# Two blocks of a feed-forward layer regrouped into one seven-product matrix scheme, with a fixed order by half step on VectorE, ScalarE and the DMA queue

## Chip, cores and metric

The kernel runs on one core of one Trainium2 chip. The metric is device microseconds of an execution. One profiled execution comes with its span, from the first to the last instruction.

## What is computed

A chunked attention over 4 x 8 heads with 768 positions of 64 (chunks of 32 queries, each against 8 memory keys and 56 neighbours) gives 3072 tokens of 512 features. Two feed-forward layers follow, in 32-bit floats:

```python
x = attention(q, k, v, mem_k, mem_v)          # 3072 x 512
h = x @ w_in                                  # 512 x 2048
g = maximum(h, 0) + log1p(exp(-abs(h)))       # softplus
x = g @ w_out                                 # 2048 x 512
h = x @ w_in2
g = h - tanh(h)
out = g @ w_out2
```

## The kernel before, in words

**Numbers.** Every operand of the feed-forward products is split into a high part, rounded to the format that TensorE takes at full rate (fp32r), and a low rest. A product is three matmuls, high-high, high-low and low-high (`mm3`, L307). Splitting costs a cast on ScalarE and a subtraction on VectorE per tile.

**Attention.** A unit is 128 tokens; there are 24. `s_mm` (L202) makes scores, `softmax` (L217) normalises, `t_mm` (L251) transposes, `t_out` (L259) copies the transposes, `v_mm` (L265) multiplies by values, `x_out` (L280) splits the result into an x tile. All units share the PSUM tile ps_a.

**Layer one** works on six blocks j of 512 tokens. For each of 16 slices f of the 2048 features, `ff_h` (L316) makes h with 12 matmuls into one of two banks ps_h, `chain1` (L332) takes softplus, cast (gh) and subtraction (gl), and two slices later (LAG) `ff_y1` (L359) adds the slice's part to the four banks ps_y with 12 matmuls. I call 12 such matmuls a half step; TensorE alternates between an h and a y half step. Weights w0 to w15 stay on chip in split form; slices 7 and 15 share a place from block one on (`load_w1`, L161), so that w15 is free for raw data. After the last slice `out1` (L366) writes the block's y to DRAM.

Block 0 runs in an opening with an order written out by hand (`OPENING`, L44) for TensorE, VectorE and ScalarE. From block 1 on only TensorE's order is that of the program (L623). The other engines and SP, which issues all DMAs, are ordered by a planner from its own estimates and from priorities: `hp(HPC)` ahead for the softplus chain, `hp(HPA)` for attention, `hp(HPJ)` behind for jobs.

During block j, `piece` (L708) puts the four attention units of block j + 1 between half steps, one every 8 (ATT_STEP), scores at k, transposes 4 later, values 8 later together with the next unit's scores; each block starts and ends its own run of four. `work` (L617) runs one of 20 jobs every four slices: `job_w` (L384) unpacks a 1 MB piece of layer two's weights, makes the seven operand sums of the scheme, splits them and writes them to DRAM; `job_x` (L410) does the same for layer one's outputs. Their tiles come from the pool `o` with four buffers.

**Layer two** takes 1024 tokens (TB) at a time, three times. Each of its two products is cut into 2 x 2 quarters and made by a scheme with seven products in place of eight. `h_phase` (L531) makes 7 products for each of 8 pairs p of feature slices, 6 matmuls each; `y_phase` (L563) makes 7 products over 8 p with 2 x 3 matmuls each and, on the way, casts and subtracts g and forms differences of g in place. Weights come through a ring of five 1 MB slots (`Ring`, L480) from DRAM, split x by `x2_load` (L456).

Of the kernel before, what the change touches and what calls it, by code (L numbers as in the profile page):

```python
# [20 lines left out]
P = 128  # L21
# [7 lines left out]
KT = DM // P  # L29
# [7 lines left out]
ATT_STEP = 8  # L37
# [31 lines left out]
SHARED = (7, 15)  # L69
EXP_BIAS = 2.0 ** -112  # L70
# [3 lines left out]
def attention_ffn_ffn(  # L74
# [36 lines left out]
    wod = dpool.tile([P, 7, NP, 2, HALF], F32, name="wod")  # L111
# [4 lines left out]
    zeros = const.tile([P, 512], BF16, name="zeros")  # L116
# [21 lines left out]
    def split_w(raw, f, kinds="io", t=None):  # L138
# [20 lines left out]
        weights["slot", f] = t  # L159
# [120 lines left out]
    def x_out(u):  # L280
        src = att.pop(u)["x"]
        x = x_tile(u // UB)
        o = (u % UB) * P
        xh, xl = (x[:, :, s, o : o + P].rearrange("p (a b) t -> p b a t", b=2) for s in range(2))
# [4 lines left out]
    def at_do(u, r):  # L289
        with hp(HPA):  # L290
            if r == 3:
                v_mm(u - 1, ps_a)
                s_mm(u, ps_a)
                run(x_out(u - 1))
                run(softmax(u))
            elif r == 0:
                s_mm(u, ps_a)
                run(softmax(u))
            elif r == 1:
                t_mm(u, ps_a[:, 0, :])  # L300
                t_out(u)
            else:
                v_mm(u, ps_a)
                run(x_out(u))

# [10 lines left out]
    def ff_h(f, slot, x, low_last=False):  # L316
        ps = ps_h[slot % 2][:, :N]
# [13 lines left out]

    def chain1(key, ps, hi_eng):  # L332
        t = tpool.tile([P, N], F32, name="t")
        if key[1]:
            nc.scalar.activation(out=t, in_=ps, func=AF.Softplus)  # L335
            yield from split_g(key, t, hi_eng)
            return
# [28 lines left out]
    def out1(j):  # L366
        for e in range(KT):
            o = opool.tile([P, N], F32, name="o")
            if e % 2:
                nc.vector.tensor_copy(out=o, in_=ps_y[e][:, :N])  # L370
            else:
                nc.scalar.copy(out=o, in_=ps_y[e][:, :N])
            nc.sync.dma_start(out=y1d[j // 2][e % 2][:, j % 2, e // 2], in_=o)

    def split_to(src, dst, shape):
        hi = opool.tile([P, *shape], F32R, name="o")
        lo = opool.tile([P, *shape], F32R, name="o")
        nc.scalar.copy(out=hi, in_=src)  # L378
        nc.vector.tensor_tensor(out=lo, in0=src, in1=hi.bitcast(F32), op=ALU.subtract)  # L379
        for s, t in ((0, hi), (1, lo)):  # L380
            for at, n, place in dst(s):
                nc.sync.dma_start(out=place, in_=t[:, at : at + n].bitcast(F32))

    def job_w(kind, p):  # L384
        src = w2i if kind == "i" else w2o
        raw = wpool.tile([P, 4 * HALF, 2], U32, name="w15")
        nc.sync.dma_start(out=raw.rearrange("p n two -> p (n two)"), in_=src[p].bitcast(U32))
        yield
        lo, hi = raw[:, :, 0], raw[:, :, 1]
        c = opool.tile([P, 4 * HALF], U32, name="o")  # L390
        nc.scalar.mul(c.bitcast(F32), hi.bitcast(F32), EXP_BIAS)
        nc.vector.tensor_scalar(out=c, in0=c, scalar1=3, scalar2=None, op0=ALU.logical_shift_left)
        for of, k, op in ((hi, 0x80000000, ALU.bitwise_and), (lo, 29, ALU.logical_shift_right)):
            nc.vector.scalar_tensor_tensor(  # L394
                out=c, in0=of, scalar=k, in1=c, op0=op, op1=ALU.bitwise_or
            )
        w = c.bitcast(F32).rearrange("p (i n) -> p i n", i=4)

        def place(s, a, n):
            return wid[p][:, a : a + n, s] if kind == "i" else wod[:, a : a + n, p, s]  # L400

        split_to(w[:, 1:4], lambda s: ((0, 2, place(s, 0, 2)), (2, 1, place(s, 6, 1))), [3, HALF])
# [5 lines left out]
        split_to(w, lambda s: ((0, 4, place(s, 2, 4)),), [4, HALF])  # L408

    def job_x(b, e):  # L410
        raw = wpool.tile([P, 2, 2, N], F32, name="w15")
        nc.sync.dma_start(out=raw, in_=y1d[b][e])
        yield
        b11, b21, b12, b22 = raw[:, 0, 0], raw[:, 0, 1], raw[:, 1, 0], raw[:, 1, 1]

        def put(q, src):
            o = opool.tile([P, 2, N], F32R, name="o")
            nc.scalar.copy(out=o[:, 0], in_=src)
            nc.vector.tensor_tensor(
                out=o[:, 1], in0=src, in1=o[:, 0].bitcast(F32), op=ALU.subtract  # L420
            )
            nc.sync.dma_start(out=x2d[b][q - 1][:, e], in_=o.bitcast(F32))

        def minus(out, x, y):
            nc.vector.tensor_tensor(out=out, in0=x, in1=y, op=ALU.subtract)

        put(1, b11)
        put(2, b21)
        put(3, b22)
        minus(b12, b12, b11)  # L430
        put(5, b12)
        minus(b22, b22, b12)
        put(6, b22)
        minus(b11, b22, b11)
        put(7, b11)
        minus(b21, b21, b22)
        put(4, b21)
# [31 lines left out]
    def half_of_y(b, q, p):  # L469
# [4 lines left out]
        for b in range(NT)  # L474
        for u in [half_of_h(b, p, i) for p, i in h_order]
# [4 lines left out]
    class Ring:  # L480
# [5 lines left out]
        def add(self, t):  # L486
# [4 lines left out]
            _, layer, x, half = u  # L491
            if layer == "h":
                src = wid[x][:, 4 * half : 7 if half else 4]
                n = 3 - half + 1 if not half else 3
            else:
                src = wod[:, WPLACE[x], 4 * half : 4 * half + 4]
# [33 lines left out]

    def h_phase(b):  # L531
        held = {}
        for p, i in h_order:
# [10 lines left out]
            if i == 3 and p in (0, 4) and 0 < b < NT - 1:  # L544
                with hp(HPJ):
                    run(job_x(b + 1, p // 4))
            if i == 0:
                g2[p] = wpool.tile([P, 4, N], F32, name=f"w{7 + p}")
            g = g2[p]
            with hp(HPC):  # L550
# [9 lines left out]
                else:  # L560
                    tanh_rest(g[:, 2], ps)

    def y_phase(b):  # L563
        t2 = [wpool.tile([P, 4, N], F32, name=f"w{i}") for i in (5, 6)]
        held = {}
        for i, q in enumerate(PRODUCTS):
            ps = [banks[(2 * b + d) % 4][i % 2] for d in range(2)]
            for p in range(NP):
# [17 lines left out]
                if p == NP // 2 and b + 1 < NT:  # L586
                    x2_load(b + 1, q)
            with hp(HPC):
                for d in range(2):
# [10 lines left out]
                    t0 = b * TB + N * (q in (3, 7))  # L600
                    nc.sync.dma_start(out=out[e][:, t0 : t0 + N], in_=o)
# [11 lines left out]
    jobs = [("i", p) for p in range(NP)] + [(0, e) for e in range(2)]  # L613
    jobs += [("o", p) for p in range(NP)] + [(1, e) for e in range(2)]
    jobs = [job_w(*x) if isinstance(x[0], str) else job_x(*x) for x in jobs]

    def work():  # L617
        if jobs:
            with hp(HPJ):
                for _ in jobs.pop(0):  # L620
                    pass

    with tc.manual_schedule(engines={mybir.EngineType.PE}):  # L623

        with tc.manual_schedule(engines={mybir.EngineType.DVE, mybir.EngineType.Activation}):
# [15 lines left out]
            first = wpool.tile([P, 2, 2, 512], F32R, name="w0")  # L641
            raws.update((str(f), raw) for raw, f in w1.staged)
# [8 lines left out]
            for token in OPENING.split():  # L651
# [20 lines left out]
                elif op == "H":  # L672
                    going["c", i] = chain1((1, 0, i), ff_h(i, i, x_tile(0), i == 0), nc.scalar)
# [19 lines left out]
        for f in SHARED:  # L693
            raw = weights["slot", f]
            nc.sync.dma_start(out=w1d[f], in_=raw.bitcast(F32))

        pend = [(0, NF - LAG + i) for i in range(LAG)]
        for j in range(1, NB):
            x = x_tile(j)
            todo = {}  # L700
            if j + 1 < NB:
                for i in range(UB):
                    u, k = UB * (j + 1) + i, ATT_STEP * i
                    todo[k] = u, 3 if i else 0
                    todo[k + 4] = u, 1
                todo[k + 6] = u, 2

            def piece(k):  # L708
                if k in todo:
                    u, r = todo[k]  # L710
                    at_do(u, r)
                    if r == 2:
                        u += 1
                    if r > 1 and u + 1 < NU:
                        at_load(u + 1)

            for f in range(NF):
                ps = ff_h(f, slot, x)
                with hp(HPC):
                    run(chain1((1, j, f), ps, nc.scalar))  # L720
                piece(2 * f)
                pend.append((j, f))
                if len(pend) > LAG:
                    run_y()
                piece(2 * f + 1)
                slot += 1
                if f == SHARED[0] + LAG:
                    load_w1(SHARED[1])
                elif f == LAG - 1 and j > 1:
                    load_w1(SHARED[0])  # L730
                if f % 4 == 3:
                    work()
                if j == NB - 1:
                    if f == 0:
                        attention.close()
                        lpool = ctx.enter_context(
                            tc.tile_pool(name="l2", bufs=1, reuse_waits="tile")
                        )
                        pool = ctx.enter_context(
                            tc.tile_pool(  # L740
                                name="psb", bufs=1, space=bass.MemoryType.PSUM, reuse_waits="tile"
                            )
                        )
                        ps_b = tuple(pool.tile([P, 512], F32, name=f"ps_b{e}") for e in range(2))
                        slots = [
                            x_tile(NB - 2).rearrange("p k s n -> p (k s n)")[:, i : i + 2048]
                            for i in (0, 2048)
                        ]
                        slots.append(lpool.tile([P, 2048], F32R, name="ring"))
                        slots += [  # L750
# [76 lines left out]
```

## Time and profile before

| | |
|---|---|
| median of 3 runs | 1076.71 us (1074.69 to 1077.01) |
| the profiled execution | 1074.53 us |
| its span | 1072.8 us |
| instructions | 18489 |
| TensorE, VectorE, ScalarE busy | 1054.3, 669.0, 551.9 us |
| granted TensorE clock, mean | 1.000 |
| moved by DMA | 258.11 MB, mean 241 GB/s |

Durations below are of the one profiled execution, whose own time stands beside its span. An engine's busy share is an average over stages; the rows by stage tell more. A helper that records many operations shows one line for all of them, so L309 is nearly every matmul, and the tile's name says which one. `PEld` is TensorE's weight load, which runs beside its matmuls. A group of rows written as `out<-in` names tiles without their numbers.

### The profile page before, as it was taken

The page shows a single profiled execution, that of the slowest core. Times are in us where ns is not written, and L with a number is a line of the kernel's source. Part 1 is how long each engine was busy: PE and PEld are TensorE (multiplying, and loading weights), DVE is VectorE, ACT ScalarE, POOL GpSimd, SP SyncE. Part 2 cuts the span into 40 slices and gives each one's busy share as a digit, 9 for nine tenths or more (in the row PEclk, how much of TensorE's full clock was granted, in tenths as well). Part 3 has the DMA queues.
Part 4 walks back from the last instruction along what each step waited for, and adds up shares of the span by engine and source line. Part 5 has one row for each costly group of instructions (what it writes and reads, how often), then busy time and mean ns, then how long its engine had stood idle before and what let it go on. Part 6 is the DMA issues. An engine that isn't in the chain of part 4 may idle for free.

```text
span 1072.8 us, 18489 instructions
## 1 busy us (share of the span) xinstructions
PE 1054.3 (98%) x7491; PEld 863.8 (81%) x7493; DVE 669.0 (62%) x1026; ACT 551.9 (51%) x914; POOL 0.7 (0%) x6
## 2 busy tenths in 40 slices
PE   6899999999999999999999999999999999999998
PEld 5677888888888888888888888888888888888886
DVE  6999657536635564673344456785676976456954
ACT  5898555545535554564334454454554554444453
POOL 0000000000000000000000000000000000000000
PEclk9999999999999999999999999999999999999999
DMA  9972258838736765874599865986799986555651
GB/s 378 407 286 70 85 181 263 258 101 276 271 109 223 290 233 179 251 228 142 192 331 326 288 220 197 361 326 241 240 344 330 363 323 233 183 173 215 233 214 60
DMA packets 75509, 258.11 MB, mean 241 GB/s; under 512 B 6560, under 2 KB 35232, under 8 KB 60064
## 3 DMA queue, kind: packets, MB, share of 16 engines
q1 hardware_dynamic: 75424, 256.93, 68.1%
q8 instruction: 59, 0.97, 0.4%
q14 instruction: 26, 0.21, 0.1%
HBM read 190.84 MB, written 66.06 MB: 239 GB/s over the span
## 4 chain that ended last, share of the span: by engine, by line
PE 83%; DVE 13%; ACT 2%; issue 1%; DMA 0%; ACTq 0%
PE ps_y L309 37%; PE ps_h L309 31%; PE ps_b L309 10%; DVE w L524 4%; DVE gl L524 2%; DVE o L147 2%; PE ps_a L273 2%; PE ps_a L209 1%; DVE w L156 1%; DVE o L145 1%; PE ps_a L254 1%; DVE t L342 1%; DVE gl L356 1%; ACT sm L238 0%; ACT o L143 0%
## 5 line engine op out<-in xcount | busy, mean ns | idle before, releaser
L309 PE MATMUL ps_h<-x,w 128*128 128x512 f32 x1140 | 275.3, 390 | 2.3 <-DVE w L156 1.6
L309 PE MATMUL ps_y<-gh,w 128*128 128x512 f32 x768 | 256.7, 396 | 0.0
L309 PEld LDWEIGHTS ps_h<-x,w 128*128 128x128 f32 x1140 | 213.2, 188 | 48.1 <-DVE w L156 2.6
L309 PEld LDWEIGHTS ps_y<-gh,w 128*128 128x128 f32 x768 | 144.1, 188 | 31.2
L573 ACT CAST gh<-w 128x512 fp32r<-128x512 f32 x168 | 104.7, 624 | 106.3 <-DVE gl L524 66.2
L524 DVE TENSOR_TENSOR gl<-w,gh 128x512 fp32r<-128x512 f32 x168 | 115.2, 690 | 60.4 <-ACT gh L573 59.9
L309 PE MATMUL ps_y<-gl,w 128*128 128x512 f32 x384 | 150.0, 391 | 1.2 <-DVE gl L356 1.2
L356 DVE TENSOR_TENSOR gl<-t,gh 128x512 fp32r<-128x512 f32 x96 | 66.0, 688 | 115.4 <-ACT gh L352 113.9
L335 ACT ACTIVATE t<-ps_h 128x512 f32<-128x512 f32 x80 | 47.8, 597 | 125.7 <-PE ps_h L309 125.3
L309 PE MATMUL ps_y<-w,x 128*128 128x512 f32 x402 | 94.2, 389 | 0.0
L309 PEld LDWEIGHTS ps_y<-w,x 128*128 128x128 f32 x402 | 75.5, 188 | 15.7
L309 PEld LDWEIGHTS ps_y<-gl,w 128*128 128x128 f32 x384 | 72.2, 188 | 16.4 <-DVE gl L356 2.5
L528 ACT ACTIVATE tanh<-sum 128x512 f32<-128x512 f32 x72 | 45.5, 632 | 65.2 <-DVE sum L520 65.0
L309 PE MATMUL ps_h<-gh,x 128*128 128x512 f32 x176 | 68.5, 389 | 0.0
L309 PE MATMUL ps_b<-gh,x 128*128 128x512 f32 x176 | 68.5, 389 | 0.0
L379 DVE TENSOR_TENSOR o<-o 128x768 fp32r<-128x768 f32 (+1 forms) x32 | 34.9, 1091 | 44.1 <-DMA wod<-o 17.0
L352 ACT CAST gh<-t 128x512 fp32r<-128x512 f32 x96 | 59.7, 623 | 3.8 <-DVE t L342 2.1
L309 PE MATMUL ps_h<-w,x 128*128 128x512 f32 x234 | 59.4, 389 | 0.0
L378 ACT CAST o<-o 128x768 fp32r<-128x768 f32 (+1 forms) x32 | 30.1, 941 | 48.8 <-DVE o L394 34.0
L309 PE MATMUL ps_y<-gh,x 128*128 128x512 f32 x176 | 54.9, 389 | 0.0
L309 PEld LDWEIGHTS ps_h<-w,x 128*128 128x128 f32 x234 | 43.9, 188 | 9.1
L524 DVE TENSOR_TENSOR w<-sum,tanh 128x512 f32<-128x512 f32 x72 | 49.2, 684 | 1.0
(123 smaller groups left out, 1406.2 us busy)
## 6 DMA issues: line engine op xcount, KB each, us to landing
x<-wod SPq DMA_DIRECT2D x33, 1024.0 KB, 4.8
x2d<-o SPq DMA_DIRECT2D x42, 512.0 KB, 6.3
x<-wid SPq DMA_DIRECT2D x21, 1024.0 KB, 6.1
w<-x2d SPq DMA_DIRECT2D x21, 1024.0 KB, 7.2
qk<-in_qk SPq DMA_DIRECT2D x22, 768.0 KB, 6.1
x<-wid SPq DMA_DIRECT2D x18, 768.0 KB, 6.0
v<-in_vv SPq DMA_DIRECT2D x22, 512.0 KB, 4.5
w<-w1d SPq DMA_DIRECT2D x9, 1024.0 KB, 7.1
```

The source lines that it names most:

```text
L145: nc.vector.tensor_scalar(out=c, in0=c, scalar1=3, scalar2=None, op0=ALU.logical_shift_left)
L147: nc.vector.scalar_tensor_tensor(out=c, in0=src, scalar=k, in1=c, op0=op, op1=ALU.bitwise_or)
L273: nc.tensor.matmul(out=ps[h : h + 64, p % 2, 2 * P + t0 : 2 * P + t0 + CHUNK], lhsT=a["v"][r, c, p, :], rhs=a["pT"][r, p, CHUNK * c : CHUN ...
L309: nc.tensor.matmul(out=ps, lhsT=a, rhs=b, start=first and i == 0, stop=last and i == 2, skip_group_check=on,)
L335: nc.scalar.activation(out=t, in_=ps, func=AF.Softplus)
L352: nc.scalar.copy(out=gh, in_=t)
L356: nc.vector.tensor_tensor(out=gl, in0=t, in1=gh.bitcast(F32), op=ALU.subtract)
L378: nc.scalar.copy(out=hi, in_=src)
L379: nc.vector.tensor_tensor(out=lo, in0=src, in1=hi.bitcast(F32), op=ALU.subtract)
L524: nc.vector.tensor_tensor(out=out, in0=x, in1=y, op=ALU.subtract)
L528: nc.scalar.activation(out=t, in_=h, func=AF.Tanh)
L573: nc.scalar.copy(out=gh, in_=src)
```

## The change

**Stages.** Blocks 0 to 3 of layer one stay as they are. Blocks 4 and 5 go together: all their h first, in 32 half steps (block 5 three slices behind block 4), softplus written straight to the tiles g2 (for the second block less the first, where the scheme wants the difference), then y for 1024 tokens by `y_phase` with layer one's weights, 7 x 8 x 2 x 3 matmuls. h rotates over six banks (ps_y and ps_h) after the first four half steps. `PHASES` is this y stage and then the three pairs of stages of layer two.

**Weights.** At the end of the opening `keep_w1` writes the split weights to DRAM: 16 pieces of 512 KB for h, 24 of 256 KB for y. `t_load` brings h weights back, 1 MB for two slices, five slots. `job_w1` makes the sums of layer one's output weights, eight jobs. The ring carries layer one's y weights too.

**Attention.** Units 8 to 23 follow one another in `ATT_ORDER`, every 6 half steps, through blocks 1 to 3. Units 20, 21 and 22 (of block 5, whose x tile is still in use) go to DRAM (`x1d`) and come back in one 1.5 MB load.

**Order.** From block 1 to the end of the two-block h stage VectorE, ScalarE and SP also run in program order. `tick` is called once each half step, 130 times; it lists what each engine does in it: late DMA writes, loads, the softmax steps, one step of each active job, then the softplus chain. Jobs are generators with a `yield` at each half step, four half steps (LEAD) between load and use. `JOBS` gives their start ticks, weight jobs every 3 ticks in the two-block stage, every second one in places of its own (SECOND). `defer` puts a DMA write into the next tick or later. From tick 130 on jobs run as before.

```diff
-ATT_STEP = 8
+ATT_STEP = 6
+ATT_ORDER = (8, 9, 10, 11, 20, 12, 13, 14, 15, 21, 16, 17, 18, 19, 22, 23)
+VIA_DRAM = (20, 21, 22)
+PLAIN = NB - 2
+T_LAG = 3
+LEAD = 4
+T_RING = 5
+FIXED = 130
+GSLOT = (8, 9, 10, 11, 12, 13, 14, 7)
+JOBS = (
+    (1, 15, 24, 43, 53, 76, 85, 94),
+    (5, 14, 23, 33, 66, 75, 84, 94, 97, 100, 103, 106, 109, 112, 118, 158),
+    (42, 54, 163, 170, 216, 228),
+)
+SECOND = (97, 103, 109)
+PHASES = ((1, NT - 1),) + tuple((2, b) for b in range(NT))
...
     def split_to(src, dst, shape):
         hi = opool.tile([P, *shape], F32R, name="o")
+        nc.scalar.copy(out=hi, in_=src)
+        yield
+        put(hi, dst(0))
         lo = opool.tile([P, *shape], F32R, name="o")
-        nc.scalar.copy(out=hi, in_=src)
         nc.vector.tensor_tensor(out=lo, in0=src, in1=hi.bitcast(F32), op=ALU.subtract)
...
+        defer(put, lo, dst(1))
...
+    def job_w1(p):
+        c = tpool.tile([P, 4, HALF], F32, name="c2", bufs=1)
+        a, b = (
+            weights["slot", f][:, 1].bitcast(F32).rearrange("p s (i n) -> p i s n", i=2)
+            for f in (p, p + NP)
+        )
+        for out, x in ((c[:, 1:2], a[:, 0:1]), (c[:, 0:1], a[:, 1:2]), (c[:, 2:4], b)):
+            nc.vector.tensor_tensor(out=out, in0=x[:, :, 0], in1=x[:, :, 1], op=ALU.add)
+        sums(c)
+        yield
+        yield from split_to(c, lambda s: ((0, 4, wod[0][:, 2:6, p, s]),), [4, HALF])
...
+    def tick(chain=iter(())):
+        k = now[0]
+        now[0] += 1
...
+        calls, late[:] = [x for x in late if x[0] <= k], [x for x in late if x[0] > k]
+        for _, f, args in calls:
+            f(*args)
+        i, r = divmod(k, ATT_STEP)
+        u = ATT_ORDER[i] if i < len(ATT_ORDER) else None
+        before = ATT_ORDER[i - 1] if 0 < i <= len(ATT_ORDER) else None
+        if u is not None:
+            if r == 1:
+                if i + 2 < len(ATT_ORDER):
+                    qk_load(ATT_ORDER[i + 2])
+                if 0 < i < len(ATT_ORDER) - 1:
+                    v_load(ATT_ORDER[i + 1])
+                next(soft[u])
+            elif r == 2:
+                run(soft.pop(u))
+        if r == 1 and before in VIA_DRAM:
+            run(soft.pop(("x", before)))
+        active.extend(job() for job in plan.get(k, ()))
+        for job in active[:]:
+            if next(job, active) is active:
+                active.remove(job)
+        if r == 0 and before is not None:
+            v_mm(before, ps_a)
+        if r == 0 and u is not None:
+            s_mm(u, ps_a)
+        if r == 4 and u is not None:
+            t_mm(u, ps_a[:, 0, :])
+        next(chain, None)
...
+        run(chain)
...
-        for j in range(1, NB):
+        for j in range(1, PLAIN):
             x = x_tile(j)
...
+                ps = ff_h(f, ps_h[slot % 2], x)
+                tick(chain1((1, j, f), ps, nc.scalar))
                 pend.append((j, f))
...
+                run_y()
...
+                tick()
...
+        for n, (t, f) in enumerate(steps):
+            ps = ps_h[(slot + n) % 2] if n < 4 else (*ps_y, *ps_h)[(n - 4) % 6]
+            weights["i", f] = w1t["i", f]
+            ff_h(f, ps, xs[t])
+            if f < NP and not t:
+                g2[f] = g_tile(f)
+            g = g2[f % NP][:, 2 * (f // NP) + t]
+            tick(act_g(g, ps, g2[f][:, 0] if t and f < NP else None))
...
+        fixed.close()
 
         banks = [ps_b, tuple(ps_h), tuple(ps_y[:2]), tuple(ps_y[2:])]
-        for b in range(NT):
-            h_phase(b)
+        for b, (layer, _) in enumerate(PHASES):
+            if layer == 2:
+                h_phase(b)
             y_phase(b)
```

## Rows read from the trace of the kernel before

**Rows 1.** The page: busy us, share of the span and instructions of each engine.
```profile
PE 1054.3 (98%) x7491; PEld 863.8 (81%) x7493; DVE 669.0 (62%) x1026; ACT 551.9 (51%) x914; POOL 0.7 (0%) x6
```
**Rows 2.** Busy us by stretch: PE, PEld, DVE, ACT, POOL, granted clock, DMA share, GB/s.
```profile
80.00:120.00 40.00, 39.75 (x414) 31.97 (x413) 38.62 (x48) 30.35 (x59) 0.00 (x0) 1.00 0.21 73
...
225.00:323.00 98.00, 98.00 (x915) 80.34 (x914) 53.89 (x84) 48.04 (x66) 0.00 (x0) 1.00 0.63 205
...
518.00:610.50 92.50, 92.50 (x410) 76.62 (x409) 39.87 (x58) 34.91 (x55) 0.00 (x0) 1.00 0.85 295
...
686.00:763.00 77.00, 76.88 (x339) 63.17 (x338) 55.60 (x88) 36.88 (x60) 0.00 (x0) 1.00 0.77 280
763.00:839.00 76.00, 76.00 (x337) 62.94 (x336) 53.41 (x86) 41.81 (x73) 0.00 (x0) 1.00 0.93 332
```
**Rows 3.** Chain of waits in layer one: start us, length us, what.
```profile
130.14 0.79 PE ps_a L209 x53
130.93 2.99 PE ps_y L309 x12
...
153.46 1.06 PE ps_a L273 x64
...
155.31 2.96 PE ps_y L309 x12
...
221.03 1.07 PE ps_a L273 x64
...
599.60 2.72 PE ps_h L309 x12
...
610.48 1.36 PE ps_b L309 x6
```
**Rows 4.** TensorE's waits, longest in total: us, times, longest us.
```profile
PE ps_a L209 <- DMA qk<-in_qk: 5.0, 1, 5.0
```
**Rows 5.** Chain of waits in layer two: start us, length us, what.
```profile
690.06 0.60 DVE gl L524
...
1068.30 0.69 PE ps_h L309 x3
```
**Rows 6.** Groups of instructions by line: count, busy us and mean ns, idle before.
```profile
L335 ACT ACTIVATE t<-ps_h 128x512 f32<-128x512 f32 x80 | 47.8, 597 | 125.7 <-PE ps_h L309 125.3
L573 ACT CAST gh<-w 128x512 fp32r<-128x512 f32 x168 | 104.7, 624 | 106.3 <-DVE gl L524 66.2
L524 DVE TENSOR_TENSOR gl<-w,gh 128x512 fp32r<-128x512 f32 x168 | 115.2, 690 | 60.4 <-ACT gh L573 59.9
L394 DVE SCALAR_TENSOR_TENSOR o<-w,o 128x1024 uint32<-128x1024 uint32 x32 | 39.1, 1222 | 0.6
L405 DVE TENSOR_TENSOR o<-o 128x256 f32<-128x256 f32 x16 | 6.8, 424 | 0.4
L379 DVE TENSOR_TENSOR o<-o 128x768 fp32r<-128x768 f32 (+1 forms) x32 | 34.9, 1091 | 44.1 <-DMA wod<-o 17.0
L378 ACT CAST o<-o 128x768 fp32r<-128x768 f32 (+1 forms) x32 | 30.1, 941 | 48.8 <-DVE o L394 34.0
L243 ACT ACT_TABLE_LOAD x16 | 20.5, 1283 | 0.3
```
**Rows 7.** Timeline of ScalarE, 628 to 642 us: start us, us, operation, idle before.
```profile
636.84 0.62 ACT L573 CAST gh<-w 128x512 fp32r<-128x512 f32 x1
```
**Rows 8.** Waits from 127.5 to 610 us: us in total, times, longest us.
```profile
DVE o L379 <- DMA wid<-o: 15.5, 6, 4.0
...
ACT o L418 <- DMA wod<-o: 8.5, 3, 4.3
```
**Rows 9.** DMA issues: count, KB each, median us to landing.
```profile
w<-in_w1i SPq DMA_DIRECT2D x16, 512.0 KB, 10.6
...
wid<-o SPq DMA_DIRECT2D x16, 512.0 KB, 5.2
...
wid<-o SPq DMA_DIRECT2D x16, 256.0 KB, 6.3
```

More of the change, by code (lines that the diff above doesn't have):

```diff
@@ L329, in ff_h, with softplus @@
         return ps
+    def softplus(out, x):
+        nc.scalar.activation(out=out, in_=x, func=AF.Softplus)
     def chain1(key, ps, hi_eng):
@@ new lines, in job_x, with high, low @@
+    def job_x(b, e, second=False):
+        raw = wpool.tile([P, 2, 2, N], F32, name="w6" if second else "w15")
+        nc.sync.dma_start(out=raw, in_=y1d[b][e])
+        for _ in range(LEAD):
+            yield
+        b11, b21, b12, b22 = raw[:, 0, 0], raw[:, 0, 1], raw[:, 1, 0], raw[:, 1, 1]
+        o = {}
+        def high(q, src):
+            o[q] = opool.tile([P, 2, N], F32R, name="o"), src
+            nc.scalar.copy(out=o[q][0][:, 0], in_=src)
+        def low(q):
+            t, src = o.pop(q)
+            minus(t[:, 1], src, t[:, 0].bitcast(F32))
+            defer(put, t, ((0, 2, x2d[b][q - 1][:, e]),))
+        high(1, b11)
+        high(2, b21)
+        yield
+        low(1)
+        low(2)
+        high(3, b22)
+        yield
+        low(3)
@@ L490, in add @@
             self.at[u] = t
-            _, layer, x, half = u
-            if layer == "h":
+            b, what, x, half = u
+            if what == "h":
                 src = wid[x][:, 4 * half : 7 if half else 4]
@@ L543, in h_phase @@
             ring.done()
-            if i == 3 and p in (0, 4) and 0 < b < NT - 1:
-                with hp(HPJ):
-                    run(job_x(b + 1, p // 4))
             if i == 0:
-                g2[p] = wpool.tile([P, 4, N], F32, name=f"w{7 + p}")
+                g2[p] = g_tile(p)
             g = g2[p]
@@ L611, in run_y @@
                 out1(j)
[L613 to L618, printed above, removed]
-            with hp(HPJ):
-                for _ in jobs.pop(0):
-                    pass
-    with tc.manual_schedule(engines={mybir.EngineType.PE}):
-        with tc.manual_schedule(engines={mybir.EngineType.DVE, mybir.EngineType.Activation}):
+    plan, now, active, late = {}, [0], [], []
@@ new lines, in attention_ffn_ffn, with defer @@
+    soft = {}
+    def defer(f, *args, more=0):
+        if now[0] < FIXED:
+            late.append((now[0] + more, f, args))
+        else:
+            f(*args)
+    def tick(chain=iter(())):
+        k = now[0]
+        now[0] += 1
+        if k >= FIXED:
+            while active:
+                run(active.pop(0))
+            with hp(HPJ):
+                for job in plan.get(k, ()):
+                    run(job())
+            return
+        calls, late[:] = [x for x in late if x[0] <= k], [x for x in late if x[0] > k]
+        for _, f, args in calls:
+            f(*args)
+        i, r = divmod(k, ATT_STEP)
[23 more added lines that the diff above has]
+        next(chain, None)
+        if r == 4 and u is not None:
+            t_out(u)
+        next(chain, None)
+        if r == 0 and before is not None:
+            soft["x", before] = x_out(before)
+            next(soft["x", before])
+        if r == 0 and u is not None:
+            soft[u] = softmax(u)
+            next(soft[u])
+        if r == 0 and before is not None:
+            next(soft["x", before], None)
+        run(chain)
@@ L695, in attention_ffn_ffn @@
             nc.sync.dma_start(out=w1d[f], in_=raw.bitcast(F32))
+        for f in range(NF):
+            keep_w1(f)
+        fixed.enter_context(tc.manual_schedule(engines={mybir.EngineType.SP}))
         pend = [(0, NF - LAG + i) for i in range(LAG)]
-        for j in range(1, NB):
-            x = x_tile(j)
[L700 to L715, printed above, removed]
+        w1t = {}
@@ L717, in attention_ffn_ffn, with t_load @@
+        def t_load(u):
+            t = wpool.tile([P, 2, 2, 512], F32R, name=f"w{u % T_RING}")
+            nc.sync.dma_start(out=t.bitcast(F32), in_=w1id[u])
+            for i in range(2):
+                w1t["i", 2 * u + i] = t[:, i, 0], t[:, i, 1]
+        for j in range(1, PLAIN):
+            x = x_tile(j)
             for f in range(NF):
[L718 to L721, printed above, removed]
+                ps = ff_h(f, ps_h[slot % 2], x)
+                tick(chain1((1, j, f), ps, nc.scalar))
@@ L756, in attention_ffn_ffn @@
-        while pend:
-            run_y()
-        for t in slots[3:]:
-            ring.add(t)
+                run_y()
+                if f == SHARED[0] + LAG:
+                    defer(load_w1, SHARED[1])
+                elif f == LAG - 1 and j > 1:
+                    defer(load_w1, SHARED[0])
+                if j == PLAIN - 1 and 0 <= f - LAG < T_RING:
+                    defer(t_load, f - LAG)
+                tick()
+                slot += 1
+        xs = [x_tile(PLAIN), None]
+        steps = []
```

223 lines of the change are left out of this document (127 added, 96 removed).

## The prediction

> **What bounds the kernel now.** I read the page's busy shares first, then the busy times by stage, then the chain of waits, then who waited for whom. TensorE is busy 98% of the span, VectorE 62% and ScalarE 51% [rows 1], so the question is whether TensorE is ever held up. By stage it is not: a block with attention (225 to 323 us; the other three are like it), the last block of layer one and an h stage of layer two (763 to 839 us) show TensorE busy for the whole of their length, at a granted clock of 1.00; only a y stage of layer two (686 to 763 us) loses 0.12 us [rows 2]. A busy matmul record is pipelined, so the speed comes from the chain: from block one on it steps from one half step (12 matmuls of 512 columns) to the next in 2.72 us, with nothing between them in the last block of layer one [rows 3]. That is 2.72 / 12 = 0.2267 us a matmul. All waits of TensorE with a named cause lie in the opening; the longest is the first load, 5.0 us [rows 4]. So from 127 us to the end the time is a count of matmuls. Whatever takes matmuls away shortens it, unless the change makes TensorE wait.
>
> Check of that reading: layer two runs from 610.48 us [rows 3] to the last matmul at about 1068.99 us [rows 5], 458.5 us. It holds 3 x 2 x 336 = 2016 matmuls, 2016 x 0.2267 = 457.0 us; the 1.5 us over are 0.5 us for each of its three y stages, at whose start VectorE sets the pace.
>
> **The change part by part.**
>
> *Matmuls.* Two blocks' y in layer one are 2 x 16 x 4 x 3 = 384 matmuls before; the seven products need 7 x 8 x 2 x 3 = 336. The h of both blocks stays plain, 384 either way. So 48 go: 48 x 0.2267 = **-10.9 us**, all on the path. By the Trainium skill (TensorE: Matmul & The Clock Gate, section "Back-to-back issue gap") a sustained stream at 512 columns takes 131 ns a matmul and an isolated one 216 ns; this trace, at 226.7 ns, disagrees with the first and lies 11 ns above the second; by the figures the term would be 6.3 or 10.4 us. The row decides, and it leaves no chance for the first.
>
> *Attention.* Units 8 to 23 come every 6 half steps in one run rather than every 8 with a fresh start in each block. Where a block starts, scores and values stand apart today: 0.79 us for scores plus 2.99 - 2.72 on the half step behind, and 1.07 us for values plus the 0.24 that a half step behind values takes longer, 2.37 us; joined they take 1.06 + 0.79 + 0.24 = 2.09 us [rows 3]. Four such pairs become one: 3 x 0.28 = **-0.8 us**.
>
> *The new y stage* starts like those of layer two, each one cast and one or two subtractions a product: gl, plus t for products 1, 6 and 5. The chain at such a start steps through them in pieces of 0.60 us [rows 5], so 1.2 us against 6 x 0.2267 = 1.36 us of matmuls: VectorE keeps up, but for the start: **+0.5 us**.
>
> *Entry of that stage.* Its first operand is long there, but its cast and subtraction stand behind the fixed order, whose last entry is the softplus of the very last h. If they can't be taken forward, TensorE waits for softplus, cast and subtraction: 0.60 + 0.62 + 0.69 = 1.9 us [rows 6]. In layer two a cast of the coming y stage does run early: at 636.8 us for a stage that starts near 686 [rows 7]. So 0 to 1.9; I take the middle, as both orders are possible: **+1.0 us**.
>
> *Work added to VectorE and ScalarE.* Eight sums of layer one's output weights: three adds (0.42 for 256 columns twice, 0.69 for 512), four sums of 0.42, one subtraction of 1024 columns, 1.22: 4.4 us each, 35 us in all [rows 6]. A layer-two weight job costs VectorE a shift (0.69) + 2 x 1.22 + 4 x 0.42 + 2 x 1.09 = 7.0 us, an attention unit 3.8 us (five passes over 512 columns and two small ones) [rows 6]. One of the blocks 1 to 3 then holds 5.3 units, 3 such jobs, 2.7 sums and 0.7 of an x job (7.6 us): against 53.9 us today with 4 and 4 [rows 2] that is 53.9 + 5.1 + 11.7 - 2 = 69 us in about 101 us of TensorE. In the two-block h stage seven jobs take 49 us of VectorE in 92.5 us. Both fit beside TensorE: **0**; the cover is the two buffers of ps_h and the two-step lag of y, three half steps or 8.2 us before the next h needs the bank. What comes from late jobs is priced in the next part.
>
> *Fixed order.* VectorE, ScalarE and SP now run what each half step lists, in that order, ahead of that half step's softplus. Today's waits of these engines for a buffer or load are hidden: VectorE waits 15.5 us for the writes of one kind of job tile, the longest 4.0 us; ScalarE's 4.3 us are the longest of its own [rows 8]. Each is under the 8.2 us of cover, and attention has its four half steps from scores to transposes as before (10.9 us against some 5 us: four passes over 512 columns, two small ones, an exp, a table load of 1.28 [rows 6]); values now follow the transposes after two instead of four half steps, 5.4 us against a softplus and a copy of 0.6 each. SP's queue stops at each entry that isn't ready, and the loads behind it (queries, values, raw weights) wait too; a raw load has four half steps, 10.9 us, before ScalarE wants it. Two waits on top of each other, 4.0 + 4.3 us, just pass the cover of 8.2. A gain is excluded, as no wait of TensorE is there to win; so the ends are 0 and about 6 us (0.5 us in each of a dozen places). The rows are nearest to the low end: **+1.0 us**.
>
> *DMA.* 40 kept pieces (14 MiB) are written as the opening splits its weights; from 80 to 120 us the DMA engines are busy 21% of the time [rows 2]. Pieces issued at its very end delay the query load behind them, which has 12 half steps. 8 MiB of h weights, 14 of ring loads, 8 of sums and 3 of x through DRAM come on top, and 4 of shared weights go: 43 MiB or 45 MB on 258 MB. The two-block h stage moves 7 x 2.93 MB of jobs, 6 MB of weights and 1.6 MB of x, 28 MB or 306 GB/s; today's last block has 295 GB/s at share 0.85 without a wait of TensorE, the h stage of 763 to 839 us 332 GB/s at 0.93 [rows 2]. **0**, with 0 to 3 us where three x units come back by DRAM into the second block's first h: 2.5 MB at that rate are 8 us and some latency, against four half steps or 10.9 us.
>
> *Layer two* keeps its matmuls; its first h stage gets a weight job of 7 us and two x jobs; the one that has two x jobs today keeps VectorE busy 53.4 of 76 us [rows 2], so 60 of 76: **0**.
>
> Sum: -10.9 - 0.8 + 0.5 + 1.0 + 1.0 = -9.2 us. The profiled execution took 1074.53 us for a span of 1072.8; the sum makes it 1065.3. The median of the three runs is 2.2 us above it, so I forecast 1076.71 - 9.2 = **1067.5 us**.
>
> **The rivals.**
>
> *A, forecast:* matmul count less 1 to 4 us of small waits, 1064.5 to 1070.
>
> *B, part of the gain goes into waits at half steps.* A job tile that isn't free holds the cast, and behind it the softplus and the next h. The Trainium skill says that ScalarE and VectorE take their instructions strictly in order, from a queue eight deep (TensorE: Matmul & The Clock Gate, table at its head); nothing in the runs so far shows its depth. For B: x jobs allot seven tiles in six half steps with four buffers, so the fifth waits about 1.3 half steps, 3.5 us, and may meet an exp with its two table loads (3.2 us). Against: 8.2 us hold both. If it passes the cover by 0.5 to 1 us in eight places, 4 to 8 us: 1070 to 1074.5.
>
> *C, slower: the tiles of the jobs bound the two-block h stage.* Seven jobs come three half steps (8.2 us) apart, each sending four tiles through four buffers. A tile lives at most for a cast (0.94), a subtraction (1.09) and its write [rows 6]; with the 5.2 to 6.3 us that such writes take to land today [rows 9] that is 7.2 to 8.3 us, just in step. From 6.2 us on each job slips, and the slips add up; the last job has three half steps of margin before y starts. At 10.6 us, what the loads of the crowded opening took [rows 9], it is 4.4 x 7 = 31 us less 8.2: 23 us, and a time near 1090. It decides against the change from a landing of about 8.8 us, where 2.6 x 7 - 8.2 = 10 us eat the gain. Against: the load of that stage, above, is that of stages in which nothing waits.
>
> *D, no gain:* the same slip near 8.8 us, or a stalled entry plus B: 1074.6 to 1078.8.
>
> **How the numbers follow.** A 0.66, B 0.16, D 0.07, C 0.11. A measurement of this kernel can tell about 0.2%, 2.15 us, from no change. A and nearly all of B are faster by more: 0.81; D with B's edge 0.08; C 0.11. The range takes A with its bounds, the matmuls' and attention's terms alone (1076.7 - 11.7 = 1065.0, less half a us of spread between runs), and B's upper end: 1064.5 to 1074.0; C and D, 0.18, are left out.
>
> **What the changed profile would show.** Right: chain pieces of 2.72 us from block one to the entry of the new y stage, then 76 to 77 us of six-matmul turns of 1.36 us; layer two's first matmul near 601 us; TensorE's waits outside the opening a few us in all. A wait at the entry of 1.5 to 2 us whose releaser is a gl would put that term at its upper end. Wrong by B: waits of matmuls on ps_h for softplus, or transposes on sm, spread over 130 to 430 us. Wrong by C: ScalarE or VectorE waiting for DMA on job tiles in the h stage, growing from job to job, and a long wait of the first y product. The forecast falls if the chain has DMA or ScalarE stretches of over 5 us after 127 us, or if the granted clock falls below 1.00 in a stage behind such a wait.

## The result, and the profile after

The changed kernel takes 1066.01 us (median of 4 runs, 1064.96 to 1069.10) against 1076.15 us of the kernel before (median of 4): ratio 0.9912, 95% interval 0.9888 to 0.9936. It is faster by 10.1 us. The profiled execution's span went from 1072.8 to 1063.5 us. The forecast was 1067.5 us, with a range of 1064.5 to 1074.0.

The busy shares on the changed kernel's page, which answer to [rows 1]:

```profile
PE 1046.6 (98%) x7445; PEld 856.6 (81%) x7445; DVE 734.6 (69%) x1149; ACT 573.8 (54%) x949; POOL 0.7 (0%) x6
```

VectorE has 65.6 us more to do, TensorE 7.7 us less busy, and TensorE is still at 98%. Busy times by stage of the changed kernel, columns as in [rows 2]; the stages are the end of the opening, a stretch with attention, the two-block h stage, layer one's new y stage, and layer two's first h and y stage:

```profile
80.00:120.00 40.00, 39.75 (x415) 32.01 (x414) 38.52 (x48) 30.35 (x59) 0.00 (x0) 1.00 0.90 318
...
225.00:323.00 98.00, 98.00 (x1097) 80.64 (x1081) 56.58 (x98) 54.55 (x78) 0.00 (x0) 1.00 0.73 249
434.00:524.00 90.00, 89.97 (x397) 74.18 (x396) 64.08 (x91) 38.18 (x55) 0.00 (x0) 1.00 0.99 349
524.00:601.00 77.00, 76.21 (x335) 62.51 (x334) 51.59 (x78) 38.91 (x65) 0.00 (x0) 1.00 0.90 326
601.00:677.00 76.00, 75.84 (x335) 62.46 (x334) 59.42 (x95) 45.15 (x77) 0.00 (x0) 1.00 0.90 322
677.00:754.00 77.00, 76.84 (x338) 63.01 (x337) 55.58 (x88) 37.41 (x61) 0.00 (x0) 1.00 0.89 338
```

The kept weights fill the end of the opening (DMA share 0.90 where it was 0.21) without costing TensorE anything there: 39.75 us busy, as before. The two-block h stage runs the DMA engines at 0.99, and TensorE still works through it. From 120 us to the end only two waits of its matmuls have a named cause (total us, times, longest):

```profile
PE ps_b L317 <- DVE gl L583: 0.7, 1, 0.7
PE ps_y L317 <- DVE sum L579: 0.2, 1, 0.2
```

Two waits of its weight loads (PEld) before the y stage matter too, one for a softplus in the two-block stage, one for a copy of y that itself waited for a tile of the pool `o`:

```profile
PEld ps_y L317 <- ACT w L340: 0.5, 1, 0.5
PEld ps_y L317 <- DVE o L381: 0.4, 1, 0.4
```

How near to the edge the two-block stage is, the waits of ScalarE and VectorE in it tell (434 to 526 us; total us, times, longest). In [rows 8] the longest were 4.0 us for VectorE and 4.3 us for ScalarE.

```profile
ACT o L388 <- DMA wod<-o: 15.3, 4, 4.4
ACT o L388 <- DMA y1d<-o: 8.4, 1, 8.4
...
DVE o L392 <- DMA wod<-o: 7.2, 5, 2.2
DVE o L392 <- DMA y1d<-o: 5.6, 1, 5.6
```

These are casts and subtractions that wait until an earlier tile of the pool `o` has been written out. The chain of waits no longer runs along TensorE here, but along such writes (start us, length us), although TensorE loses next to nothing in this stage:

```profile
440.28 9.15 DMA y1d<-o
...
467.09 9.44 DMA wod<-o
478.20 8.14 DMA wod<-o
```

Stage by stage, TensorE's first matmul of the new y stage starts at 522.97 us, and layer two's first moved from 610.32 to 600.57 us, by 9.75 us; its last ends 9.1 us earlier, as layer two takes 0.6 us longer. The first and the last of these rows bound the y stage, the second is the one wait of its matmuls with a cause:

```profile
522.97 0.39 PE L317 MATMUL ps_b<-gh,ring 128*128 128x512 f32 x1
...
528.50 0.50 PE L317 MATMUL ps_b<-gl,ring 128*128 128x512 f32 x1 [0.71 <-DVE gl L583]
...
600.57 1.52 PE L317 MATMUL ps_y<-w,x 128*128 128x512 f32 x6
```

### The profile page after: what moved, and what is told of

Read it like the earlier page. It is cut to its first block, busy times and chain, and to the rows that moved or that the text cites. A ratio compares the mean times of both kernels' runs of the same rounds, so it can differ in the third digit from the quotient of the medians.

```text
span 1063.5 us, 18633 instructions
## 1 busy us (share of the span) xinstructions
PE 1046.6 (98%) x7445; PEld 856.6 (81%) x7445; DVE 734.6 (69%) x1149; ACT 573.8 (54%) x949; POOL 0.7 (0%) x6
## 2 busy tenths in 40 slices
DMA packets 99542, 303.20 MB, mean 285 GB/s; under 512 B 7808, under 2 KB 54912, under 8 KB 81792
## 4 chain that ended last, share of the span: by engine, by line
PE 70%; DVE 15%; DMA 11%; ACT 2%; issue 2%; SPq 0%; ACTq 0%; DVEq 0%
PE ps_y L317 32%; PE ps_h L317 24%; PE ps_b L317 11%; DVE w L583 5%; DMA w<-in_w1i 4%; DMA wod<-o 3%; DVE gl L583 3%; PE ps_a L290 2%; DVE o L164 2%; PE ps_a L226 1%; DVE o L392 1%; DMA w<-in_w2o 1%; DMA w<-in_qk 1%; DMA qk<-in_qk 1%; DMA y1d<-o 1%
## 5 line engine op out<-in xcount | busy, mean ns | idle before, releaser
L317 PE MATMUL ps_h<-x,w 128*128 128x512 f32 x900 | 216.9, 391 | 0.7 <-DVE t L353 0.5
L317 PE MATMUL ps_y<-gh,w 128*128 128x512 f32 x512 | 172.9, 399 | 0.0
L317 PEld LDWEIGHTS ps_y<-gh,w 128*128 128x128 f32 x512 | 96.1, 188 | 21.4 <-DVE o L381 0.4
L317 PE MATMUL ps_y<-gh,x 128*128 128x512 f32 x352 | 109.4, 389 | 0.0
L317 PE MATMUL ps_y<-gl,w 128*128 128x512 f32 x256 | 100.1, 391 | 1.2 <-DVE gl L367 1.2
L317 PEld LDWEIGHTS ps_y<-gh,x 128*128 128x128 f32 x352 | 66.1, 188 | 13.7
L388 ACT CAST o<-c 128x1024 fp32r<-128x1024 f32 (+1 forms) x34 | 33.0, 969 | 76.2 <-DVE c L433 32.4
L317 PE MATMUL ps_y<-gl,x 128*128 128x512 f32 x176 | 68.7, 390 | 0.2
L583 DVE TENSOR_TENSOR w<-w 128x512 f32<-128x512 f32 x88 | 59.4, 684 | 11.0 <-DMA w<-y1d 6.4
L317 PE MATMUL ps_y<-x,w 128*128 128x512 f32 x240 | 55.5, 390 | 0.0
L317 PE MATMUL ps_b<-w,x 128*128 128x512 f32 x216 | 54.8, 389 | 0.0
```

Of the source, the lines that this page charges most:

```text
L317: nc.tensor.matmul(out=ps, lhsT=a, rhs=b, start=first and i == 0, stop=last and i == 2, skip_group_check=on,)
```

## The experiments

**Is the gain the 48 matmuls?** The last product of the new y stage is made twice; its quarter of layer one's output comes out doubled.

```diff
+                    if b == 0 and q == 4:
+                        mm3(ps[d], wh, wl, gh, gl, False, False, True)
                     mm3(ps[d], wh, wl, gh, gl, p == 0 and q in (1, 2, 5), p == NP - 1, q in (6, 7, 3, 4))
```

> The last of the seven products of layer one's new y stage is made twice (48 matmuls more, the number that the change takes away; that quarter of the output comes out doubled). Theory (from 127 us on the time is a count of matmuls): 48 x 0.2267 = 10.9 us above the changed kernel, 1076.9 us, all of it in the stretch from 523 us to layer two's first matmul, 88.5 us in place of 77.6; no other stage changes its length by over 0.5 us. Rival (in that stage VectorE, ScalarE or the ring's loads set the pace, and matmuls have room): under 5 us, 1066 to 1071.

1077.72 us (median of 10), 1.0007 of the kernel before (0.9995 to 1.0020), 11.7 us above the changed kernel: the whole gain is gone. The y stage runs from the first to the second of these rows:

```profile
525.50 0.39 PE L317 MATMUL ps_b<-gh,ring 128*128 128x512 f32 x1
...
614.14 1.52 PE L317 MATMUL ps_y<-w,x 128*128 128x512 f32 x6
```

That is 88.64 us in place of 77.60, so 11.0 us for 48 matmuls that count 10.9: the stage has no spare room. That no other stage would change by over 0.5 us was wrong. The opening took 0.9 us longer, a softplus held TensorE for 1.7 us in the two-block stage, and layer two took 0.7 us less.

**What is the fixed order worth?** First the changed kernel with everything but TensorE left to the planner, the softplus chain under `hp(HPC)`, jobs under `hp(HPJ)`.

```diff
-        fixed.enter_context(tc.manual_schedule(engines={mybir.EngineType.SP}))
+        fixed.close()
...
```

> The changed kernel, but VectorE, ScalarE and the DMA queue are left to the planner from block one on, with the priorities of the kernel before around the softplus chain and the jobs. Theory (the gain is the matmul count; the order only keeps waits inside the cover of 8.2 us, as the planner did before): 1064 to 1070 us, with TensorE's waits between 127 and 523 us under 4 us. Rival (at a DMA share of 0.99 in the two-block stage only the written order keeps the jobs in step): 1072 to 1085 us, with waits of TensorE on ps_h, ps_y or gl between 430 and 530 us.

1068.64 us, ratio 0.9924 (0.9902 to 0.9947), span 1065.9. TensorE has one wait with a cause after the opening, in the blocks with attention:

```profile
PE ps_a L271 <- DVE sm L266: 2.3, 1, 2.3
```

In the two-block stage and at the entry of the y stage the planner lost nothing (90.00 us busy of 90 from 434 us, 77.00 of 77 from 524 us, where the written order has 76.21). So the regrouping brings some 8 of the 10 us under either order. The written order's share is 2.6 us by the medians, and the two intervals overlap, so it isn't clear of noise; the traces place it at the transpose that waited, after which the planner's run also lost some clock (0.98 granted from 260 to 330 us).

Then the order alone: all six blocks plain, 160 half steps in fixed order, weight and x jobs by a table of mine.

```diff
-PLAIN = NB - 2
+PLAIN = NB
...
-FIXED = 130
...
+FIXED = 160
...
-PHASES = ((1, NT - 1),) + tuple((2, b) for b in range(NT))
+PHASES = tuple((2, b) for b in range(NT))
```

> The fixed order and attention every 6 half steps, without the regrouping: all six blocks of layer one plain, no kept pieces, no sums, jobs spread over blocks one to five. Theory: the matmuls are those of the kernel before, so its time less the joined attention pieces (0.2 to 0.8 us) plus small waits: 1074.5 to 1077.5 us; layer two starts at 609.5 to 612 us. Rival (part of the gain comes from the order itself): 1066 to 1073 us.

1093.69 us, ratio 1.0159 (1.0138 to 1.0180): neither the theory nor the rival. TensorE's waits with a cause after 120 us, and the copy on VectorE behind one of them in the timeline (start us, length us, idle before):

```profile
PE ps_y L317 <- DVE o L381: 13.5, 3, 6.4
```

```profile
249.32 0.69 DVE L381 COPY o<-ps_y 128x512 f32<-128x512 f32 x1 [6.99 <-DMA y1d<-o]
```

L381 copies a finished y out of ps_y into a tile of `o`. My table let a weight job hold a tile of that pool at that moment, so the last of the four copies waited 6.99 us for an earlier copy's write, and the next y couldn't start. With the start half steps moved clear of the three places where a block's y is copied out (which puts two weight jobs into layer two's first h stage):

```diff
-    (5, 12, 19, 26, 33, 64, 71, 78, 85, 92, 99, 106, 135, 142, 149, 156),
-    (42, 53, 113, 124, 218, 230),
+    (5, 11, 17, 31, 63, 69, 75, 81, 95, 101, 107, 143, 149, 155, 163, 167),
+    (42, 52, 114, 132, 218, 230),
```

> The run with the fixed order alone (no regrouping), with the jobs' start half steps moved so that no job holds tiles of the pool o when a block's four y tiles are copied out (two weight jobs moved behind, into layer two's first h stage). Theory (the three waits of 13.5 us in the run before came from that table, not from the order as such): TensorE's waits under 3 us from 127 to 620 us and 1074.5 to 1079 us, within 0.2% of the kernel before. Rival (the fixed order costs by itself): again over 1085 us.

1075.65 us, ratio 0.9990 (0.9977 to 1.0003), and no wait of TensorE before layer two. The order and the joined attention by themselves are worth 0.1%, by the interval 0.2% at most. But the order hangs on its table: with the first choice of start half steps it lost 17 us.

**How long may ScalarE wait before TensorE notices?** Each job's raw load is issued later, nearer to its first use, all else in its half step; without a lead, then with two half steps.

```diff
-LEAD = 4
+LEAD = 0
...
-    (5, 14, 23, 33, 66, 75, 84, 94, 97, 100, 103, 106, 109, 112, 118, 158),
+    (9, 18, 27, 37, 70, 79, 88, 98, 101, 104, 107, 110, 113, 116, 122, 158),
...
```

> The changed kernel with each job's raw load issued in the half step that uses it in place of four half steps earlier (15 weight jobs and 2 x jobs in the fixed part; all later steps of the jobs stay in their half steps). ScalarE then waits some 7 to 8.4 us for each load, ahead of the softplus of that half step. Theory (the cover is three half steps, 8.2 us, less the softplus, in blocks one to three, and five half steps in the two-block stage): each of the 10 jobs of blocks one to three costs 0 to 1.5 us, those of the two-block stage nothing but their sum at the end; 1066 to 1082 us. Rival (a wait over one half step goes to TensorE at once): (7.5 - 2.7) x 17 = 80 us, about 1146.

1150.87 us, ratio 1.0690 (1.0664 to 1.0715). The rival's time, but not for its reason. Timeline of one load:

```profile
192.84 1.12 ACT L408 ACTIVATE c<-w 128x1024 f32<-128x1024 f32 x1 [9.77 <-DMA w<-in_w2i]
...
203.46 1.09 PE L271 MATMUL ps_a<-ident,sm 128*128 128x128 f32 x4 [3.61 <-DVE sm L266]
```

ScalarE stood 9.77 us; TensorE went on through it and stopped later, 3.61 us, at the transposes of the unit whose exp had stood behind it. The loads kept ScalarE for up to 14.6 us, not for 7 to 8.4. TensorE's waits with a cause add up to 62.0 us of the 84.9 us lost; the granted clock was 0.87 to 0.97 in the stretches with these waits.

> As the run without a lead, but with each job's raw load two half steps before its use in place of four (or none). ScalarE should wait about 2 to 5 us for each of 17 loads. Theory (cover of about 8 us before TensorE notices; the run without a lead was slow because its loads kept ScalarE for 9.8 to 14.6 us, not because the cover is smaller): TensorE's waits from 127 to 530 us are under 5 us and the time is 1065 to 1071 us. Rival (any wait of over one half step goes to TensorE): 20 us or more, 1085 us and above.

This is the run with two half steps. 1077.79 us, ratio 1.0009 (0.9992 to 1.0025), lies between theory and rival: my theory's numbers failed here too. The timeline of the worst case, SP's issue, ScalarE and TensorE:

```profile
346.93 0.48 SPq L402 DMA_DIRECT2D w<-in_w2i  x1
...
359.77 1.12 ACT L408 ACTIVATE c<-w 128x1024 f32<-128x1024 f32 x1 [12.00 <-DMA w<-in_w2i]
...
361.91 1.93 PE L290 MATMUL ps_a<-pT,v 64*64 64x32 f32 x64 [4.49 <-ACT pT L279]
```

The load took 12.8 us, not 7 or 8: in the 4 us before it, on the same queue, SP had issued a shared weight, queries, values and four y writes. The cover that gave way was the shorter one, values two half steps behind their transposes: 12.00 - 4.49 leaves 7.5 us. So most of a wait stays hidden, about 6 to 7.5 us in these two cases. Two half steps of lead are too few and four are enough; three were not tried. That this load was slow because of what stood before it is the likely reading, not one that a run tested. The Trainium skill says that on each DMA engine descriptors are consumed in ring order (DMA: Bandwidth & Descriptors, section "Queues, rings and completion order"); the row agrees with that, but doesn't show single engines. The other waits of this run are 3.6 us for a softplus in the two-block stage and 2.0 us for a ring load in the y stage.

**Where does the 0.7 us at the y stage's entry come from, and can it go?** The last weight job of the stage is moved into the y stage.

```diff
-    (5, 14, 23, 33, 66, 75, 84, 94, 97, 100, 103, 106, 109, 112, 118, 158),
+    (5, 14, 23, 33, 66, 75, 84, 94, 97, 100, 103, 106, 109, 112, 140, 158),
```

> The changed kernel with the last weight job of the two-block stage started in half step 140, in the y stage, in place of 118. Theory (the wait of 0.7 us at the entry of the y stage comes from that job's passes on VectorE, which stand before the stage's second gl): the wait goes, VectorE's new job in the y stage is hidden, 1064 to 1066 us. Rival (the wait is that of softplus, cast and subtraction behind the fixed order's last entry, as the prediction had it): 0.5 to 1.9 us of wait at the entry stay. Second rival (the y stage has no room on VectorE, which runs two subtractions a product): 1067 us or more.

1075.92 us, ratio 0.9994 (0.9978 to 1.0011). At the entry my theory was right: TensorE has no wait with a cause from 522 to 580 us. The moved job, though, now runs inside the y stage, and 1.2 us on ps_b came up there after 580 us, as the second rival said of its room. Then a longer wait, far behind, took the gain, and the forecast time was missed. TensorE's waits, and the stretches of the y stage and around the long wait (columns as in [rows 2]):

```profile
PE ps_y L317 <- DVE gl L583: 7.2, 1, 7.2
PE ps_b L317 <- DVE gl L583: 1.2, 1, 1.2
```

```profile
522.00:580.00 58.00, 58.00 (x256) 47.47 (x255) 43.79 (x66) 31.03 (x50) 0.00 (x0) 1.00 0.87 307
580.00:601.00 21.00, 19.84 (x88) 16.12 (x87) 11.22 (x17) 8.10 (x13) 0.00 (x0) 1.00 0.95 337
682.40:689.70 7.30, 0.12 (x1) 0.00 (x0) 5.57 (x11) 2.31 (x4) 0.00 (x0) 0.66 0.80 327
689.70:692.00 2.30, 2.28 (x5) 1.82 (x6) 2.30 (x5) 0.00 (x0) 0.00 (x0) 0.50 0.97 305
692.00:694.00 2.00, 2.00 (x6) 1.59 (x5) 2.00 (x5) 0.62 (x1) 0.00 (x0) 0.50 0.95 334
```

At 682.4 us layer two's first y stage has begun, but VectorE and ScalarE are still at passes of the second x job, which wait for tiles to be written, and the planner had put them ahead of the stage's gl. In the changed kernel that job is through when the stage starts.

Next the planner from the two-block stage on, since it had lost nothing there.

```diff
+        fixed.close()
         for n, (t, f) in enumerate(steps):
...
```

> The changed kernel with the fixed order ended at the start of the two-block h stage; from there the planner orders VectorE, ScalarE and the DMA queue. Theory: the fixed order's worth of some 2.4 us against the planner comes from one wait of a transpose in blocks one to three (2.3 us), so it stays, and the 0.7 us at the entry of the y stage go, as in the run with the planner throughout: 1064.5 to 1066.5 us, span 1062 to 1063.5. Rival (the written order is what keeps the crowded two-block stage in step): waits of TensorE from 434 to 530 us above 2 us, 1068 us or more.

1074.96 us, ratio 0.9987 (0.9971 to 1.0003): the entry of layer one's y stage has no wait, but 5.5 us came up at the same place in layer two, where passes of the second x job again stood among the stage's own. Both kernels were then given an earlier start of those x jobs.

```diff
-    (42, 54, 163, 170, 216, 228),
+    (42, 54, 160, 166, 216, 228),
```

> The changed kernel with the two x jobs of layer two's first h stage started in half steps 160 and 166 in place of 163 and 170. Theory (in two runs a slip of the second of them into the entry of the next y stage cost 5.5 and 7.2 us, in the changed kernel it ends just before): it ends some 8 us earlier, and the stage's small waits go; 1064.5 to 1066.5 us. Rival (the planner's placing of these jobs depends on all else and moves any way): a wait of over 2 us at the entry of layer two's first y stage, 1068 us or more.

> The run with the planner from the two-block stage on, with the x jobs of layer two's first h stage in half steps 160 and 166 in place of 163 and 170. Theory (its 5.5 us of wait at the entry of layer two's first y stage came from the second x job, whose passes and writes stood ahead of the stage's second gl): the wait goes with the earlier start, 1063.5 to 1066.5 us. Rival (what the planner gains at one entry it loses at another): a wait of over 2 us at that entry or at the next, 1068 us or more.

On the changed kernel 1066.26 us, ratio 0.9903 (0.9886 to 0.9921), the same time: layer two's first h stage has no wait left (76.00 us busy of 76), the 0.7 us at the entry of layer one's y stage stayed, and a softplus held TensorE for 1.1 us in the two-block stage. With the planner 1073.62 us, ratio 0.9976 (0.9963 to 0.9989): the long wait became several of 0.5 to 2.5 us, at the entries of both y stages and for a ring load of layer two. That rival held. None of these beats the changed kernel.

**Is the two-block stage at the DMA engines' limit?** Each low part that a job makes from half step 94 on is written twice, the second time to a place that nobody reads.

```diff
         defer(put, lo, dst(1))
+        if 94 <= now[0] < FIXED:
+            n = shape[0]
+            again = dpool.tile([P, *shape], F32, name=f"again{len(agains)}")
+            agains.append(again)
+            defer(put, lo, ((0, n, again),))
...
```

> The changed kernel, and each low part that a job of the two-block h stage writes is written a second time, to a place of its own that nobody reads (14 writes of 384 or 512 KB, 6.4 MB). Theory (the stage stands at the edge of what the DMA engines move, share 0.99 at 349 GB/s, and TensorE is held up only from there on): 6.4 MB are 18 us of all DMA engines; less the cover of some 8 us the entry of the y stage or the last h wait some 5 to 15 us, 1071 to 1082 us. Rival (transfers can slip without anyone noticing): TensorE's waits up to the y stage stay under 2 us, 1065 to 1068 us.

1086.69 us, ratio 1.0099 (1.0080 to 1.0118), 20.7 us above the changed kernel, more than either forecast. My count of the added writes was wrong: the DMA issues (count, KB each, median us to landing) are 18, not 14.

```profile
again<-o SPq DMA_DIRECT2D x10, 512.0 KB, 7.4
...
again<-o SPq DMA_DIRECT2D x8, 384.0 KB, 5.0
```

That is 8.4 MB, not 6.4, or 24 us at 349 GB/s. The stage itself:

```profile
434.00:524.00 90.00, 83.65 (x357) 67.19 (x356) 57.38 (x81) 34.60 (x49) 0.00 (x0) 0.98 1.02 369
```

TensorE loses 6.35 us in it, 2.65 us in the y stage, where a ring load came late, and 5.7 us in layer two's first y stage, at a gl. Its waits with a cause make 15.4 us; the rest goes with a granted clock of 0.98, 0.98 and 0.96 in these three stages. So the cover here was all but used up. Whether the DMA engines or the tiles ran out stays open: a tile now stays taken until its second write has landed too, and VectorE waited 12.8 us for such second writes. A run that moves the same bytes from tiles outside the pool `o` would tell the two apart.

## Why the prediction was right, step by step

- **What bounds the kernel:** right. Counting matmuls gave the gain, and putting 48 back took it away (1077.72 us).
- **Matmuls, -10.9 us:** right; the doubled product made its stage 11.0 us longer. By the 131 ns of the Trainium skill (TensorE: Matmul & The Clock Gate, section "Back-to-back issue gap") 48 matmuls would take an estimated 6.3 us; the run decides against it.
- **Attention, -0.8 us:** right. From the first scores to the end of the work that follows, the time over 2.72 us a half step is 480.34 - 161 x 2.72 = 42.4 us before (130.14 to 610.48 us) and, from 130.06 us to the y stage at about 523.1, 393.0 - 129 x 2.72 = 42.2 us after. That is 0.2 us less and not 0.8, but the 0.6 between are not attention's: they are the two weight loads that waited (a half step of 3.03 us where its like takes 2.77, and four of 11.37 where others take 11.04), and belong to the fixed order.
- **Work added to VectorE and ScalarE, 0:** right in time. VectorE was busy 188.48 of the 306.70 us from 127.3 to 434 us, some 62 us in 101 where 69 were counted.
- **The new y stage and its entry, +1.5 us:** it took 522.97 to 600.57 us, 77.6 against 336 x 0.2267 = 76.2 us: +1.4. Nearly all of it lies at the entry: the 21st matmul starts at 528.84 us, 1.3 us late, and 0.71 of that is put down to a gl. The mechanism at the entry was half right: casts were taken forward, and the first three slice pairs had their operands; the wait met the fourth pair, 18 matmuls in, behind VectorE's late passes of the last job. Moving that job into the stage removed it, and cost 1.2 us later in the stage and 7.2 us in layer two.
- **Fixed order, +1.0 us:** +0.6, the two weight loads above. The first is the shared pool again (a copy of y behind a tile's write, as in the order-only run), the second a softplus that stood behind a job's cast, which had waited 4.4 us for a tile. Against the planner the medians even show a gain of 2.6 us, not clear of noise, where I had excluded one: "no wait of TensorE is there to win" holds for the kernel before, and in the new one the planner did leave a wait of 2.3 us.
- **The cover of 8.2 us:** half right. 6 to 7.5 us stayed hidden where loads came late; the shorter distance from transposes to values, which I named with 5.4 us and then costed by ScalarE's 1.2 us of work, is what broke first.
- **DMA, 0:** right in time, wrong in room. I counted 28 MB and 306 GB/s; the stage moved 349 GB/s x 90 us = 31 MB at share 0.99. ScalarE's longest wait for a tile grew to 8.4 us, and single writes took up to 9.4 us on the chain, past the 8.8 us from which rival C was to decide; the cover held all the same, but for 0.33 us. 8.4 MB more made it slower than the kernel before. The traffic itself was counted well: 45 MB more, 303.20 against 258.11.
- **Layer two, 0:** +0.6 us, and with little margin: the x jobs beside its first h stage end some 4 us before the y stage; slipped, they cost 5.5 and 7.2 us.
- **The sign by which the forecast was to fall:** it showed, and the forecast held. The chain has DMA stretches of up to 9.4 us in the two-block stage and one of 10.7 us in the y stage. It follows what ended last, here backwards from waits of TensorE of 0.7 and 0.2 us; a long stretch on it doesn't say how long TensorE stood. TensorE's own waits were the sign to name.

The sum of forecast terms was -9.2 us, the last matmul came 9.1 us earlier, and the median moved by 10.1 us. The large terms were right one by one. That the sum agrees to 0.1 us is luck: 0.4 us too much for the order and 0.1 for the y stage and its entry make up for 0.6 too little for layer two.

## What to carry to other kernels

Where TensorE has no waits, count its instructions: a scheme that removes 48 of them gives their time back, if the stages that pay for it (sums, writes, reloads) keep their cover. Then look at what the cover is made of: in the stage with the DMA engines at 0.99 and TensorE at 100%, 8.4 MB more cost 20.7 us, and not in that stage alone. A written order is good where tile lifetimes were counted into it; change one entry and look at every shared pool again.

## What the runs showed of the hardware that was not expected

A wait costs more than its length. After the 7.2 us wait above TensorE was granted 0.50 of its clock, 1.2 GHz, from 689.7 to 694 us: from 689.72 to 695.01 us it started 12 matmuls, 5.3 us where 12 x 0.2267 = 2.7 would do, so some 2.6 us on top. In the run without a lead the mean granted clock of the execution fell to 0.969. And 1 MB loads of one kind on one queue, the raw weights in that same run, took anything from 5.7 to 13.1 us to land.
